# Infini-attention with a 2-D Fourier filter: stacks by 16-partition transfers, maxima eleven heads ahead, an output projection of 14 products

## The chip, the cores and the metric

The kernel runs on one core of one Trainium2 chip. The metric is the device time of one execution in microseconds, the median of the runs. A core has TensorE (PE for its products, PEld for its weight loads), VectorE (DVE), ScalarE (ACT), GpSimd (POOL) and SyncE (SP, which issues most transfers), and 16 DMA engines that carry the transfers of all issue queues.

## The reference

Two independent computations, whose results stand side by side in the output. `A` is an attention with a compressive memory, `B` filters in the frequency domain.

```python
# A: B=1, S=2048, D=576, H=32 heads of Dh=18, N=4 segments of L=512
q,k,v = heads(x@wq), heads(x@wk), heads(x@wv)
phi = lambda t: where(t > 0, t + 1, exp(t))
M, z = 0, 0
for s in range(N):
    p     = softmax(qs @ ks.T * Dh**-0.5 + mask)       # causal inside a segment
    a_dot = p @ vs
    a_mem = (phi(qs) @ M) / (phi(qs) @ z + 1e-6)
    o     = g * a_mem + (1 - g) * a_dot                # g = sigmoid(beta), one per head
    M    += phi(ks).T @ vs;   z += sum(phi(ks))
y_a = concat_heads(o) @ wo
# B: x is 2048 x 576
y_b = irfft2(rfft2(x) * (w_r + 1j*w_i))
```

## The kernel before

**Precision.** Products that need float32 are made of several passes: each operand is split into a high part with a short mantissa and the rest, a low part, and high x high, high x low and low x high are added up. The scores are made in one bfloat16 product of 108 rows: q and k are each split into three bfloat16 parts, and a *stack* holds six blocks of 18 rows (one block for each pair of parts), for eight heads and the 512 columns of a segment. Rows 108 and 109 of the query stack hold the row's maximum in two parts; rows of -1 in the key stack take it off inside the product, so that the exponential needs no subtraction.

**Stages.** The program runs the forward transform of `B`, then the projections of `A` beside the filter's pointwise part, then the inverse transform beside the first part of the attention (`prologue`), and then the attention. `projections` runs, for each of four segments, nine units of `qk_unit` (128 columns of q or k each, 1152 in all; the fifth unit, `mt==4`, is half q and half k) and four of `v_unit`. A `qk_unit` writes its three bfloat16 parts to DRAM (`qkD`), phi(q) to DRAM (`pqD`), and phi(k), transposed, to the tile `pk`.

**The attention's loop.** `attention` runs 133 steps, one head a step; four heads are a group (`k`, with head `hh` in it), eight a stack (`n`), and there are 16 stacks. Step `t` holds

- `s1(t+10)`: the scores of the head ten further on, four products and a reduction to each row's maximum on VectorE. The part on the diagonal is masked on TensorE by adding a triangle (L646, reduced by a plain reduction L647) for two of the four row blocks, and by a fused mask-and-maximum on VectorE (L641) for the other two.
- `mpath(k+2)`: for a group of four heads, the maxima are split on GpSimd (L662, L663), transposed on TensorE (L666), copied (L669) and sent into rows 108 and 109 of the query stack (L672), by a transfer from ScalarE's queue two steps later. It begins in the group's second head (`hh==1`) and goes on in its fourth (`hh==3`).
- `s2(t)`: the transposed scores with the maximum taken off, the exponential on ScalarE, and GpSimd's selection of the causal part once per group (L696).
- `pv`: the products P x V of the group before, in two of four steps, and `u_dmas`, which write the sums to DRAM.
- a share of the background list `bg`: loading and splitting `wo` (`late_setup`), and for each finished segment `mixed` (the memory part `mem1`, and `combine`, which scales, adds and splits into the high part `oh` and the low part `ol`), `den` (the denominators of the next segment), and `oproj`, the output projection.

**Order.** The order on every engine's queue is that in which the Python generators emit instructions; a wait on a queue holds up everything behind it. SyncE's queue gets up to two stack, value or sum transfers a step from the lists `q` and `qu`. `stack_dmas(n, qk)` is the list of the six transfers of a stack, 18 rows each (L621). When stack `n` begins, the transfers of the query stack `n+2`, of the key stack `n+3` and of the values are appended. There are three query and four key buffers, so a query buffer comes free when the last head of stack `n-1` is through `s2`. Requests made with `later(d, ...)` go out `d` steps later.

**The output projection.** The 576 rows of `o` lie in five tiles: four of 126 rows (seven heads) and one of 72 (four heads). `oproj` makes, for each of four row blocks and two halves, 15 products (three pairs of parts by five tiles), for the first three segments. The fourth segment's projection is `last_proj`, in an order of its own.

Of the kernel before, what the change touches and what calls it, by code (L numbers as in the profile page):

```python
# [340 lines left out]
BF=mybir.dt.bfloat16  # L341
H=32; DH=18; SC=float(DH)**-0.5
# [15 lines left out]
def host_wo(w):  # L358
    o=np.zeros((126,5,D),np.float32)
    o[:,:4]=w[:504].reshape(4,126,D).transpose(1,0,2)  # L360
    o[:72,4]=w[504:]
    return o
# [21 lines left out]
class ATT:  # L384
    def __init__(s,nc,tc,io,cp,dp):
# [6 lines left out]
        s.qkD=[d(f"qkD{i}",[1152,3,512],BF) for i in range(4)]  # L392
        s.pqD=[None]+[d(f"pqD{i}",[576,512],F32) for i in range(1,4)]
# [67 lines left out]
    def qk_unit(s,g,mt,tp,pp):  # L461
# [18 lines left out]
        if qr>r0: nc.sync.dma_start(s.pqD[g][128*mt:128*mt+qr],e[:qr])  # L480
# [5 lines left out]
        nc.sync.dma_start(s.qkD[g][128*mt:128*mt+128],sp3)  # L486
# [3 lines left out]
        n=r1-k0; c0=128*mt+k0-576  # L490
# [4 lines left out]
        nc.scalar.copy(s.pk[:,:,c0:c0+n],pt[:,:,:n])  # L495
# [99 lines left out]
    def late_setup(s,cp):  # L595
# [3 lines left out]
        s.woh=cp.tile([126,5,576],F32R,name="woh",bufs=1); s.wol=cp.tile([126,5,576],F32R,name="wol",bufs=1)  # L599
        for t in range(6):  # L600
            if t>1: yield
            if t<5:
                x=cp.tile([128,576],F32,name="ob")[:126]; q.append(x)
                nc.sync.dma_start(x,io["wo"][:,576*t:576*t+576])
            for _ in range(2): yield
            if t>0:
                x=q.pop(0)
                nc.scalar.copy(s.woh[:,t-1],x)
                nc.gpsimd.tensor_tensor(s.wol[:,t-1],x,s.woh[:,t-1].bitcast(F32),op=OP.subtract)
        yield  # L610
        yield from s.gates()
    def stack_dmas(s,n,qk):

        nc=s.nc; g,G=divmod(n,4)
        L=[]
        T,base,order=((s.Qs[n%3],0,(0,0,0,1,1,2)),(s.Ks[n%4],576,(0,1,2,0,1,0)))[qk]
        for pc,o in enumerate(order):
            a=s.qkD[g][base+8*G*18:base+8*G*18+18,o]
            ap=bass.AP(tensor=a.tensor,offset=a.offset,ap=[[1536,18],[1536*18,8],[1,512]])
            def go(T=T,pc=pc,ap=ap):  # L620
                nc.sync.dma_start(T[18*pc:18*pc+18],ap)  # L621
                if pc==5: s.loaded.add((n,qk))
            L.append(go)
        return L
# [5 lines left out]
    def s1(s,t):  # L630
# [163 lines left out]
    def mixed(s,g):  # L794
# [3 lines left out]
        for i in range(5+d):  # L798
            next(c,None); yield
            if i>=d:  # L800
                for _ in s.mem1(g,i-d): yield
# [4 lines left out]
    def combine(s,g):  # L806
# [14 lines left out]
        for t in range(7+late):  # L821
# [13 lines left out]
            if late and t>2: low(t-3)  # L835
# [288 lines left out]
```

## Time and profile before

| | us |
|---|---|
| median of three runs (726.09, 726.72, 837.55) | 726.72 |
| the profiled execution | 718.92 |
| its span, first to last instruction | 717.2 |

The granted clock of TensorE over the span is 0.997. The busiest groups of VectorE in the attention, in busy time and mean duration: the fused mask-and-maximum L641, 256 times, 141.4 us and 552 ns; the plain reduction L647, 128 times, 87.7 us and 686 ns. Of the output projection, TensorE's three groups on L849 have 120 products each. The stack transfers are 192 with 144.0 KB each.

How to read the page: "busy" is the union of an engine's instructions; matmuls are pipelined, so their mean duration is longer than the distance between two of them. A wait names the engine that was idle, the line it waited at, and what ended the wait. The chain is followed back from the last instruction through whatever released each step.

### The profile page before, as it was taken

How to read it: one execution, taken by the hardware profiler on the slowest of the kernel's cores; microseconds unless marked ns; L12 is line 12 of the kernel's file. 1: busy time of each engine (PE TensorE's matmuls, PEld its weight loads, DVE VectorE, ACT ScalarE, POOL GpSimd, SP SyncE). 2: the span in 40 equal slices, each digit the busy share in tenths (PEclk: the TensorE clock that was granted, in tenths of full speed). 3: DMA queues.
4: the chain of work that ended last, by engine and by line, in shares of the span. 5: the costliest groups of instructions: out<-in, count | busy, mean ns of one | idle time of the engine just before them, and what ended most of it. 6: DMA issues, size and time to landing. Idle time of an engine off the chain costs nothing. (4 is left out here: it accounts for less than half of the span.)

```text
span 717.2 us, 14460 instructions
## 1 busy us (share of the span) xinstructions
PE 684.1 (95%) x5007; PEld 505.7 (71%) x5007; DVE 552.3 (77%) x1270; ACT 450.1 (63%) x985; POOL 211.1 (29%) x403
## 2 busy tenths in 40 slices
PE   4999999999999999999999899899999999999997
PEld 4988869879779879999854444444466445664497
DVE  5999979899699789788588787878466876568633
ACT  3665796585586575444487677767466776567521
POOL 5432000100200111665154333435123662235300
PEclk9999999999999999999999999999999999999999
DMA  8995435645363568899547665776446775441152
GB/s 305 293 280 164 148 118 185 192 169 182 110 220 147 178 198 281 208 231 228 165 111 174 171 172 136 185 173 170 114 126 158 195 169 126 126 137 42 28 153 83
DMA packets 83304, 121.02 MB, mean 169 GB/s; under 512 B 11472, under 2 KB 50750, under 8 KB 83096
## 3 DMA queue, kind: packets, MB, share of 16 engines
q1 hardware_dynamic: 76580, 104.11, 50.3%
q0 software_dynamic: 5632, 15.76, 8.0%
q8 instruction: 39, 0.64, 0.4%
q10 hardware_dynamic: 1020, 0.25, 0.2%
q14 instruction: 33, 0.27, 0.1%
HBM read 81.78 MB, written 38.24 MB: 167 GB/s over the span
## 5 line engine op out<-in xcount | busy, mean ns | idle before, releaser
L641 DVE CUSTOM_DVE_ANT_0 junk<-s,x 128x512 bf16<-128x512 f32 (+1 forms) x256 | 141.4, 552 | 67.2 <-PE s L637 62.0
L696 POOL TENSOR_SCALAR_AFFINE_SELECT P<-P 128x512 f32<-128x512 f32 (+2 forms) x132 | 78.8, 623 | 67.3 <-ACT P L683 51.8
L647 DVE TENSOR_REDUCE mx<-s 128x4 f32<-128x512 f32 x128 | 87.7, 686 | 2.9 <-PE s L646 0.7
L683 ACT ACTIVATE P<-s 128x512 f32<-128x512 f32 x128 | 76.4, 597 | 16.5 <-PE s L682 5.4
L711 PE MATMUL pv<-P,vs 128*32 128x512 f32 (+3 forms) x1024 | 82.8, 441 | 0.0
L692 ACT ACTIVATE P<-s 128x256 f32<-128x256 f32 x128 | 49.4, 386 | 49.7 <-PE s L691 49.6
L688 ACT ACTIVATE P<-s 128x512 f32<-128x512 f32 x128 | 76.1, 594 | 2.0 <-PE s L687 1.8
L637 PE MATMUL s<-Ks,Qs 108*128 108x384 bf16 (+3 forms) x256 | 69.1, 301 | 1.2 <-DVE mx L647 0.9
L711 PEld LDWEIGHTS pv<-P,vs 128*32 128x32 f32 x1024 | 27.2, 109 | 45.3 <-issue 42.5
L459 PE MATMUL pj<-x,wqkh 128*128 128x512 f32 x162 | 56.5, 409 | 0.0
L205 DVE TENSOR_TENSOR Z<-t,t 128x290 f32<-128x290 f32 (+1 forms) x96 | 48.4, 554 | 0.1
L637 PEld LDWEIGHTS <-Qs 108*128 108x128 bf16 x320 | 31.5, 98 | 22.6 <-issue 11.3
L506 POOL MEMSET vt<- 128x32 f32 x16 | 2.4, 166 | 149.1 <-PE pm L516 127.7
L205 DVE TENSOR_TENSOR t<-Z 128x580 f32<-128x580 f32 x64 | 46.0, 755 | 0.0
L142 PE MATMUL f<-ftab,eh 128*128 128x290 f32 (+1 forms) x160 | 32.5, 322 | 12.1 <-DMA ftab<-ftab 9.5
L646 PE MATMUL s<-tri,idb 128*128 128x128 bf16 x256 | 43.2, 220 | 0.0
L295 PE MATMUL i<-civ,Y 128*128 128x256 f32 (+1 forms) x288 | 39.0, 288 | 0.2 <-POOL Y L280 0.2
L295 PEld LDWEIGHTS i<-civ,Y 128*128 128x128 f32 (+1 forms) x288 | 36.4, 181 | 1.0 <-POOL Y L280 0.4
L306 PE MATMUL i<-itab,T 128*128 128x290 f32 (+1 forms) x224 | 36.3, 305 | 0.1
L637 PE MATMUL s<-Ks,x 108*128 108x384 bf16 (+3 forms) x128 | 35.3, 306 | 1.1 <-DVE mx L647 0.6
L142 PEld LDWEIGHTS f<-ftab,eh 128*128 128x128 f32 (+1 forms) x160 | 26.2, 207 | 14.1 <-issue 8.5
L459 PE MATMUL pj<-x,wqkl 128*128 128x512 f32 x90 | 35.5, 395 | 0.0
(203 smaller groups left out, 1820.8 us busy)
## 6 DMA issues: line engine op xcount, KB each, us to landing
qkD<-sp SPq DMA_DIRECT2D x36, 384.0 KB
Ks<-qkD SPq DMA_DIRECT2D x72, 144.0 KB
x<-qkD SPq DMA_DIRECT2D x60, 144.0 KB
Qs<-qkD SPq DMA_DIRECT2D x60, 144.0 KB
xin<-xb SPq DMA_DIRECT2D x16, 384.0 KB
cfw<-cfw POOLq DMA_DIRECT2D x16, 384.0 KB, 4.4
civ<-civ POOLq DMA_DIRECT2D x16, 384.0 KB, 7.6
vs<-vD SPq DMA_DIRECT2D x16, 330.0 KB
```

What stands on the lines that cost most here:

```text
L142: nc.tensor.matmul(p[:,r,:FP],x,t,start=n==0,stop=n==6)
L205: v.tensor_tensor(o,a,b,op=op)
L295: nc.tensor.matmul(p[:m,k],Y[i][:,q,c*128:c*128+m],cc[:,hl,o:o+256],start=n==0,stop=n==5)
L459: s.nc.tensor.matmul(out,a,b,start=i==0,stop=i==len(L)-1)
L637: nc.tensor.matmul(out,Q[:108,h,128*i:128*i+128],K[:108,h,:128*(i+1)],start=True,stop=True)
L641: nc.vector.tensor_tensor_reduce(out=junk[:,:w],in0=src,in1=s.mask[:,512-w:],scale=1.0,scalar=-3.0e38, op0=OP.add,op1=OP.max,accum_out=s.m ...
L647: nc.vector.tensor_reduce(out=s.mx[k][:,hh],in_=pa.rearrange("p (b c) -> p b c",c=128),axis=mybir.AxisListType.X,op=OP.max)
L683: nc.scalar.activation(P[0][:,hh],p0,AF.Exp,scale=SC)
L688: nc.scalar.activation(P[1][:,hh],p1,AF.Exp,scale=SC)
L692: nc.scalar.activation(P[2][:,hh],p2,AF.Exp,scale=SC)
L696: nc.gpsimd.affine_select(out=x[:,r],in_=x[:,r],pattern=[[0,r.stop-r.start],[1,128]],compare_op=OP.is_ge,fill=0.0,base=0,channel_multiplie ...
L711: nc.tensor.matmul(s.pvt[32*hh:32*hh+32,128*j:],vt[:,j,19*h:19*h+32],mv[0][:,hh,mv[1]],start=j==0,stop=j>1,skip_group_check=True)
```

## The change

*Layout.* The columns of `wq` and `wk` are permuted on the host, so that a unit of 128 columns holds dimensions 0 to 15 of eight heads (dimension by dimension), and the unit `mt==4` holds dimensions 16 and 17 of all heads, of q and of k. A stack then has six blocks of 16 rows, which come from `qkD`, and twelve rows of the last two dimensions, which unit `mt==4` writes ready in order to a new DRAM tensor `reD` (six writes in place of one). The writes to `pqD` and the copies into `pk` undo the permutation by their access patterns.

*Order in the attention.* `s1` runs eleven heads ahead (the prologue eleven heads in place of ten), `mpath` begins in a group's first head and goes on in its second, and four heads (11 to 14) take the triangle and the plain reduction for all row blocks. The loads `ux` of the reciprocal's lane are asked for before its own loads, the tiles of `combine` and `mem1` are taken in the order 4, 0, 1, 2, 3, and four steps of `oproj` come ahead of `den`.

*Projection.* For the first three segments the tile of 72 rows is filled up: rows 72 to 127 of its high part and rows 72 to 87 of its low part get the low part by small copies between tiles, with matching rows of `wo`, so that its three products become two.

```diff
+ORD=(4,0,1,2,3)
 # qk_unit
-        nc.sync.dma_start(s.qkD[g][128*mt:128*mt+128],sp3)
+        if mt!=4: nc.sync.dma_start(s.qkD[g][128*mt:128*mt+128],sp3)
+        else:
+            for r,i,c,n in ((0,0,1,3),(0,1,1,2),(0,2,1,1),(64,0,3,3),(64,0,2,2),(64,0,1,1)):
+                m={3:0,2:3,1:5}[n]; a=s.reD[g][r*12//64+2*m]
+                x=sp3[r:r+64,i:i+c] if c==n else sp3[r:r+64,i:i+1].to_broadcast([64,n,512])
+                nc.sync.dma_start(bass.AP(tensor=a.tensor,offset=a.offset,ap=[[512,64],[64*512,n],[1,512]]),x)
...
-        nc.scalar.copy(s.pk[:,:,c0:c0+n],pt[:,:,:n])
+        pk=s.pk.rearrange("p a (h d) -> p a d h",d=18)
+        if mt==4: nc.scalar.copy(pk[:,:,16:],pt[:,:,:n].rearrange("p a (d h) -> p a d h",d=2))
+        else: nc.scalar.copy(pk[:,:,:16,8*mt-40:8*mt-32],pt.rearrange("p a (d h) -> p a d h",h=8))
 # stack_dmas
-            a=s.qkD[g][base+8*G*18:base+8*G*18+18,o]
-            ap=bass.AP(tensor=a.tensor,offset=a.offset,ap=[[1536,18],[1536*18,8],[1,512]])
-            def go(T=T,pc=pc,ap=ap):
-                nc.sync.dma_start(T[18*pc:18*pc+18],ap)
-                if pc==5: s.loaded.add((n,qk))
-            L.append(go)
+            a=s.qkD[g][base+128*G,o]
+            ap=bass.AP(tensor=a.tensor,offset=a.offset,ap=[[1536*8,16],[1536,8],[1,512]])
+            L.append(lambda pc=pc,ap=ap: nc.sync.dma_start(T[16*pc:16*pc+16],ap))
+        def go():
+            nc.sync.dma_start(T[96:108],s.reD[g][12*qk:12*qk+12,8*G:8*G+8])
+            s.loaded.add((n,qk))
+        L.append(go)
 # s1, red
+            if 11<=t<15:
+                nc.tensor.matmul(src[:,w-128:w],s.idb,s.tri,start=False,stop=True,skip_group_check=True)
+                nc.vector.tensor_reduce(out=s.mg[k][:,hh,i:i+1],in_=src,axis=mybir.AxisListType.X,op=OP.max)
+                return
 # combine, low
-            eng().tensor_tensor(s.ol[u][:r],s.am[u][:r],s.oh[u][:r].bitcast(F32),op=OP.subtract)
+            A,B=s.oh[u],s.ol[u]
+            l=B if u<4 else tp.tile([128,512],F32R,name="ol4",bufs=1)
+            eng().tensor_tensor(l[:r],s.am[u][:r],A[:r].bitcast(F32),op=OP.subtract)
+            if u==4:
+                s.later(1,lambda: nc.sync.dma_start(B[:72].bitcast(F32),A[:72].bitcast(F32)))
+                s.later(2,lambda: (nc.sync.dma_start(A[72:128].bitcast(F32),l[:56].bitcast(F32)),nc.sync.dma_start(B[72:88].bitcast(F32),l[56:72].bitcast(F32))))
 # oproj
-                L=[(a,b,t) for a,b in ((oh,s.woh),(oh,s.wol),(ol,s.woh)) for t in range(5)]
+                L=[(a,b,t,126) for a,b in ((oh,s.woh),(oh,s.wol),(ol,s.woh)) for t in range(4)]+[(oh,s.woh,4,128),(ol,s.wol,4,88)]
 # prologue
-        for t in range(10):
+        for t in range(11):
             for _ in s.s1(t):
-                for _ in range(1+(i%24==0)):
+                for _ in range(1+(i%5==0)):
 # attention
                     for i in range(8):
+                        if 2<i<6: s.ux_load(g-1,ORD[i-3])
                         next(r); yield
-                    for u in range(3): s.ux_load(g-1,u)
                     yield from r
                     bg.append(s.mixed(g))
-                    if g<3: bg.append(s.den(g+1,lane))
-                    bg.append(s.oproj(g-1))
+                    o=s.oproj(g-1)
+                    if g<3: bg.append(itertools.islice(o,4)); bg.append(s.den(g+1,lane))
+                    bg.append(o)
...
-            a=s.s1(t+10) if t+10<128 else iter(())
+            a=s.s1(t+11) if t+11<128 else iter(())
...
-            if hh==3 and m is not None: steps(m,1)
+            if hh==1 and m is not None: steps(m,1)
             steps(b,1)
-            if hh==3 and m is not None: steps(m,1)
-            if hh==1 and k+2<32: m=s.mpath(k+2); next(m)
+            if hh==1 and m is not None: steps(m,1)
+            if hh==0 and k+2<32: m=s.mpath(k+2); next(m)
```

The rest of the diff is the host's permutation and layout of the weights, one more row block of `wo` loaded in `late_setup`, tiles of 128 rows in place of 126, and the order 4, 0, 1, 2, 3 where tiles are loaded.

More of the change, by code (lines that the diff above doesn't have):

```diff
@@ L392, in __init__ @@
         s.qkD=[d(f"qkD{i}",[1152,3,512],BF) for i in range(4)]
+        s.reD=[d(f"reD{i}",[24,32,512],BF) for i in range(4)]
         s.pqD=[None]+[d(f"pqD{i}",[576,512],F32) for i in range(1,4)]
@@ L598, in late_setup @@
         s.sel=cp.tile([96,5,126],BF,name="sel",bufs=1); nc.gpsimd.dma_start(s.sel,io["sel"].rearrange("p (t m) -> p t m",t=5))
[L599 to L603, printed above, removed]
-                nc.sync.dma_start(x,io["wo"][:,576*t:576*t+576])
[L605 to L609, printed above, removed]
+        s.woh=cp.tile([128,5,576],F32R,name="woh",bufs=1); s.wol=cp.tile([128,5,576],F32R,name="wol",bufs=1)
+        for t in (0,1,2,3,5,4,6):
+            if t: yield
+            if t<6:
+                x=cp.tile([128,576],F32,name="ob"); q.append((t,x))
+                nc.sync.dma_start(x,io["wo"][:,576*t:576*t+576])
+            yield
+            if t!=5: yield
+            if len(q)>(t<6):
+                u,x=q.pop(0)
+                if u==5: nc.scalar.copy(s.wol[64:96,4],x[64:96]); continue
+                r=128 if u<4 else 72
+                nc.scalar.copy(s.woh[:,u],x)
+                nc.gpsimd.tensor_tensor(s.wol[:r,u],x[:r],s.woh[:r,u].bitcast(F32),op=OP.subtract)
         yield
```

52 lines of the change are left out of this document (29 added, 23 removed).

## The prediction

> **What bounds the kernel now.** I read the page first, then the busy time by stage, then the waits of TensorE in the attention, then the chain and the DMA rows of one stage, and last single rows for prices.
>
> ```profile
> span 717.2 us, 14460 instructions
> PE 684.1 (95%) x5007; PEld 505.7 (71%) x5007; DVE 552.3 (77%) x1270; ACT 450.1 (63%) x985; POOL 211.1 (29%) x403
> ```
>
> TensorE is busy 95% of the span, so time goes only where it does less work or waits less. The stages, with PE, PEld, DVE, ACT and POOL busy, clock, DMA share and GB/s:
>
> ```profile
> 80.00:280.00 200.00, 198.01 (x1128) 167.87 (x1127) 174.03 (x327) 137.52 (x272) 14.27 (x62) 1.00 0.55 181
> 280.00:345.00 65.00, 64.77 (x517) 61.48 (x516) 53.04 (x125) 30.74 (x75) 36.49 (x54) 1.00 0.84 213
> 345.00:677.00 332.00, 317.96 (x2663) 178.26 (x2662) 241.61 (x691) 226.69 (x544) 127.94 (x233) 0.99 0.55 142
> 372.00:410.00 38.00, 34.64 (x318) 17.43 (x316) 30.19 (x95) 28.25 (x69) 16.42 (x29) 1.00 0.70 171
> 410.00:440.00 30.00, 29.95 (x277) 14.82 (x268) 24.17 (x76) 23.01 (x56) 10.04 (x22) 1.00 0.56 151
> 440.00:512.00 72.00, 66.10 (x541) 32.11 (x539) 55.31 (x160) 50.70 (x121) 28.71 (x55) 0.98 0.69 170
> 677.00:717.00 40.00, 35.47 (x261) 33.44 (x261) 14.62 (x23) 8.75 (x21) 2.92 (x6) 0.99 0.34 109
> ```
>
> Projections (80 to 280) and inverse transform (280 to 345) leave TensorE idle for 2.0 and 0.2 us. The attention (345 to 677) leaves it idle 332.0 - 318.0 = 14.0 us, of which 3.4 lie in 372:410 and 5.9 in 440:512. These two are also the stages with a DMA share near 0.7, and 440:512 has the one clock below 1. What ends TensorE's waits in the attention (total, times, longest):
>
> ```profile
> PE s L682 <- DMA Qs<-mts: 3.2, 3, 1.4
> PE s L637 <- DVE mx L647: 1.5, 4, 0.6
> PE pd L765 <- DMA pq<-pqD: 1.4, 1, 1.4
> PE pb L826 <- DMA rr<-rrD: 1.2, 1, 1.2
> PE s L637 <- DMA Qs<-qkD: 0.4, 1, 0.4
> PE s L682 <- DMA x<-mts: 0.2, 1, 0.2
> ```
>
> Five of the six are transfers: 3.2 + 1.4 + 1.2 + 0.4 + 0.2 = 6.4 us. The chain of waits shows how long they take (start, duration):
>
> ```profile
> 372.67 7.55 DMA Qs<-mts
> 387.69 5.19 DMA pq<-pqD
> 392.89 8.27 DMA Qs<-qkD
> 401.24 5.59 DMA x<-mts
> 408.17 0.06 PE s L646
> ```
>
> The maxima (mts, 32 x 128 bfloat16, 8 KB) take 7.55 us, as long as a stack transfer, so they stand in a queue. The DMA rows of 410:440, where almost only stacks are loaded, show which queue (first line: busy share in 40 slices; then packets, MB and share; then issues):
>
> ```profile
> DMA  6667666666666656986566666566642002252255
> q1 hardware_dynamic: 4584, 4.43, 54.5%
> Ks<-qkD SPq DMA_DIRECT2D x12, 144.0 KB
> SPq L621 <- DMA Ks<-qkD: 12.3, 14, 1.6
> ```
>
> The last line is a wait of SP's issue queue in 345 to 700: stack issues (L621) wait for earlier stack transfers, so transfers are always pending, yet the 16 engines are pinned near 0.6. Eighteen rows divide evenly over nine engines with two rows each; 9/16 is 0.56, near the measured 54.5% and the flat run of sixes. I read it as nine full engines and seven idle ones. [...]
>
> **The change part by part.** *Stacks.* Six transfers of 18 rows become six of 16 (one row per engine) and one of 12. By rows, an engine among the nine did 6 x 2 = 12 rows per stack and now does at most 7: 7/12 of the load. The queueing part of 5 to 8 us should shrink alike, to 3 to 5 us. That bears on all DMA-ended waits.
>
> *Maxima two heads earlier.* The transpose and its store move from the fourth head of a group to the second, and the request from the second to the first, possible because the scores run one head further ahead. A pair of heads takes as long as from one P x V block (L711) to the next. Rows of this stretch (start, duration), and GpSimd groups (total, mean ns):
>
> ```profile
> 410.83 0.16 DVE L659 TENSOR_REDUCE mg<-mx 128x4 f32<-128x12 f32 x1
> 411.47 0.22 POOL L663 TENSOR_TENSOR mh<-mg,mh 128x16 bf16<-128x16 f32 x1
> 412.88 1.28 PE L711 MATMUL pv<-P,vs 128*32 128x384 f32 x16
> 416.72 0.08 DVE L641 DVE_READ_ACCUMULATOR2_ANT mg<- 128x1 f32 x1
> 416.92 0.64 PE L711 MATMUL pv<-P,vs 128*32 128x512 f32 x4
> ```
>
> ```profile
> L819 POOL TENSOR_TENSOR ol<-am,oh 126x512 fp32r<-126x512 f32 (+1 forms) x10 | 12.7, 1270 | 16.4 <-ACT oh L816 15.4 <-PE pn L784 1.0
> L832 POOL TENSOR_TENSOR am<-ux,am 126x512 f32<-126x512 f32 (+1 forms) x8 | 10.1, 1273 | 4.5 <-DVE ux L831 3.3 <-PE s L682 1.2
> ```
>
> 416.92 - 412.88 = 4.04 us, so the maxima get 4 us more, three times the longest wait for them (1.4). The 3.4 us for mts go. The waits for pq and rr go too: four steps of the output projection now stand between the last pq load and its use, and the ux loads no longer stand in the queue ahead of rr. I take all 6.4 us. What is late next is VectorE: its waits already stand in the list (1.5 us), and I give back 1.0 (bounds: 0; all 6.4).
>
> The price of the earlier transpose: TensorE takes instructions in order, and matmuls of the next head's scores and exponentials queue behind it. The last maximum of the group is now that of the first head of four, out of VectorE at 416.72 in the rows above; from the reduction L659 to the end of L663 is 411.69 - 410.83 = 0.86 us, giving 417.6. The transpose follows the P x V block that starts at 416.92 and takes 1.28 us: 418.2, a margin of 0.6. Where one of GpSimd's 1.27 us operations (L819, L832, second fence) lies in between, it is late by some 0.7. Of these 18 a quarter falls in that step: 4.5 x 0.7 = 3.2 at most; I take 1.5 (bounds 0 and 3.2).
>
> *Clock.* 440:512 ran at 0.98, costing 72 x 0.02 = 1.4 us. It is the stage with the pq wait of 1.4 us, the longest; I let it go with the wait (bounds 0 and -1.4). [...]
>
> *Products.* 3 segments x 8 tiles lose one product of 15:
>
> ```profile
> 683.70 0.83 PE L849 MATMUL po<-wol,oh 126*128 126x288 f32 x5
> 684.37 0.83 PE L849 MATMUL po<-woh,ol 126*128 126x288 f32 x5
> ```
>
> Five products start every 0.67 us, 0.134 each; 24 x 0.134 = 3.2 us. Sixteen lie in the full stages 512:560 and 600:650 and count whole, 2.1. Eight lie after 677, where the last segment's tiles wait for loads anyway (TensorE 35.5 of 40); I take 0.5 of their 1.1. So -2.6 (bounds -2.1, -3.2). The nine small copies that fill rows 72 to 127 are asked for when tile 4 is combined, which now comes first, some ten steps (20 us) ahead of its products; they cost nothing while those steps cover them.
>
> *First four heads.* Before the first P x V block VectorE sets the pace, and TensorE waits for it (L637 on L647, above):
>
> ```profile
> 356.18 0.69 DVE L647 TENSOR_REDUCE mx<-s 128x4 f32<-128x512 f32 x1
> 357.39 0.08 DVE L641 DVE_READ_ACCUMULATOR2_ANT mg<- 128x1 f32 x1
> 357.62 0.42 DVE L641 CUSTOM_DVE_ANT_0 junk<-s,x 128x256 bf16<-128x256 f32 x1
> 357.97 0.69 DVE L647 TENSOR_REDUCE mx<-s 128x4 f32<-128x512 f32 x1
> ```
>
> A head takes 1.79 us, of which 0.23 pass between the accumulator read and the next operation. A plain reduction has no such read: 4 x 0.23 = -0.9 (bound 0). The eight mask products added (0.06 each by the L646 piece of the chain, 0.5) fall in TensorE's waits.
>
> *One head moved* from the attention into the inverse transform: TensorE is full in both, so 0 (bounds: one step, 2.0, either way).
>
> *Projections.* Twenty more SP issues and a permuted copy on ScalarE:
>
> ```profile
> L621 SPq DMA_DIRECT2D Ks<-qkD x72: 265/273/468, 301.5 to 607.9; - x72
> L495 ACT COPY pk<-ptr x15: 357/588/622, 100.5 to 225.5; 128x512 f32<-128x512 f32 x12, 128x256 f32<-128x256 f32 x3
> ```
>
> Twenty issues at 0.27 us are 5.4 us of SP in 200; behind them queue the tables and inputs, loaded ahead. The copies write single words 72 bytes apart, which no row shows; if each took twice its 588 ns, ScalarE had 15 x 0.59 = 8.8 us more on 137.5 of 200. TensorE at 99% covers both. Uncovered it were +8.8; I take 0.
>
> **Sum.** -6.4 + 1.0 + 1.5 - 1.4 - 2.6 - 0.9 = -8.8 us. The profiled execution took 718.92 us (717.2 and 1.7 around it), so 710.1; the median of the runs is 726.72, 1.1% higher for no cause in the rows, and the same difference gives 717.9.
>
> **Rivals.** *A, the forecast*, 713 to 722: chance 0.61. *B, VectorE takes the place of the transfers.* Waits vanish into its own; only the products count, 726.7 - 2.6 = 724. For it: VectorE is at 55.3 of 72 in 440:512, and a head took it 1.79 of 2.02 us. Against: 410:440 ran with no transfer wait and no idle TensorE. 0.15. *C, all idle time goes*: -14.0 - 3.2 - 1.4 = -18.6, 708. For it: VectorE, too, has operands sooner. Against: a third of the listed waits is not for transfers. 0.14. *D, slower: query stacks come late.* The slot of a query stack comes free when its eighth head is done; then five steps (10.1 us) pass until its first scores instead of six, and seven transfers must be issued, not six. If 16 rows land no sooner than 18, that is one step and one issue interval (about 1 us) less: 3.1 us per stack, 13 stacks, +40, so 758. It is slower than before beyond 8.8/13 = 0.7 us per stack, and by 2% beyond 1.8. For it: the wait on Qs<-qkD exists already, with 8.27 us in the chain. Against: the 54.5%. [...] 0.08. *E*, the ScalarE copies uncovered, 727: 0.02.
>
> **Numbers.** 2%, about what a measurement here tells from no change, is 14.5 us: faster below 712.2, slower above 741.3. Only C is faster by that, 0.14; only D slower, 0.08; 0.78 within. The range 708 to 728 holds A, B, E and half of C: 0.85.
>
> **What would show it.** Right: TensorE's waits on Qs<-mts, pq and rr gone; DMA share in the attention unlike 0.56 and spread over time; stack transfers landing in 3 to 5 us in the chain; L849's successor with 336 products; idle time in the attention near 9 us (14.0 - 6.4 + 1.0 + 1.5 - 0.9). Wrong: TensorE waiting on Qs<-qkD once per stack (D), on GpSimd at the transpose once per group, on VectorE where transfers were (B), or idle in the projections (E).

## The result, and the profile after

The changed kernel takes 732.03 us (median; 730.67 to 736.75), the kernel before on the same chip 726.33 (one of its six runs took 837.55). All ratios of this document are formed over undisturbed runs alone, so that of the change, 1.0134 with a 95% interval of 1.0087 to 1.0182, isn't the quotient of these medians. It is slower, by less than 2% but clear of the noise, and outside the range given. In the experiments that follow the kernel before took 719.6 to 722.4 us (medians), so each is told by its ratio to the kernel before in the same series, with the interval.

The page of the profiled execution after, and the time by stage (columns as in the prediction's table). The two profiled executions lie 13 us apart, a little more than the ratio says:

```profile
span 730.2 us, 14514 instructions
PE 685.9 (94%) x4991; PEld 502.8 (69%) x4991; DVE 552.9 (76%) x1262; ACT 457.5 (63%) x986; POOL 209.8 (29%) x403
```

```profile
80.00:280.00 200.00, 196.64 (x1117) 166.33 (x1116) 171.84 (x322) 142.35 (x269) 14.14 (x60) 1.00 0.62 186
280.00:345.00 65.00, 63.21 (x505) 59.83 (x504) 54.85 (x125) 30.79 (x76) 35.08 (x54) 1.00 1.08 211
372.00:410.00 38.00, 29.88 (x256) 14.52 (x255) 25.14 (x80) 24.74 (x60) 16.66 (x28) 0.92 0.81 160
410.00:440.00 30.00, 28.74 (x253) 14.29 (x255) 22.77 (x70) 20.91 (x51) 8.46 (x18) 0.92 0.75 140
440.00:512.00 72.00, 65.31 (x535) 31.67 (x528) 53.32 (x158) 48.97 (x117) 27.14 (x52) 0.95 0.80 156
512.00:560.00 48.00, 48.00 (x407) 30.47 (x405) 30.97 (x90) 31.41 (x76) 13.80 (x28) 1.00 0.73 153
```

Two things stand out. The stretch 372 to 512 has become the worst: TensorE's clock is 0.92 to 0.95 there, and 410:440, which had no idle TensorE before, has some. And in the four stages shown from 280 to 512 the DMA share has risen while the GB/s have fallen (410:440: 0.56 and 151 before, 0.75 and 140 now). The transfers keep the engines busy longer for fewer bytes.

Where the time is lost shows in the times at which the same instruction runs in both traces (us from the start of each span, read from the instruction records):

```
event                                        before   after   later by
last product of the projections              282.04  283.25     1.2
last product of the inverse transform        355.35  358.77     3.4
first product of s2 of head 16               388.09  392.13     4.0
                      of head 24             406.96  418.07    11.1
                      of head 40             440.51  452.48    12.0
                      of head 56             477.32  495.04    17.7
                      of head 120            659.04  672.78    13.7
first product of the last projection         696.13  708.72    12.6
end                                          717.23  730.15    12.9
```

There are three main losses: 3.4 us up to the end of the inverse transform, 7.1 between heads 16 and 24, and 5.7 between heads 40 and 56. TensorE's waits in the attention after (total, times, longest; Qs and Ks are the buffers of the query and key stacks, x the tile that holds the first of each and the mask, mts the maxima):

```profile
PE s L702 <- ACT P L703: 6.6, 7, 4.8
PE s L653 <- DMA ux<-uD: 3.8, 1, 3.8
PE mt L686 <- POOL mh L683: 2.6, 5, 0.8
PE s L653 <- DVE mg L679: 2.0, 1, 2.0
PE s L653 <- DMA uD<-U: 1.4, 1, 1.4
PE s L653 <- DMA Qs<-qkD: 1.3, 1, 1.3
```

The waits on mts, pq and rr are gone. In their place stand single waits of 4.8, 3.8 and 2.0 us. A wait for several things carries the name of one of them, so the transfers themselves have to be looked up. The stack around the wait of 3.8 us, which ended at 465.5 (asked, landed, from the DMA records):

```
Qs<-qkD  454.81 456.04 456.62 457.26 457.91 458.55   landed 459.00 460.27 461.26 462.20 463.28 464.20
Qs<-reD  459.22                                      landed 465.19
```

It is the query stack: its seventh transfer lands at 465.19. The wait of 2.0 us ends at 485.21, and the last part of the next query stack landed at 485.02. At the wait of 4.8 us, which ended at 406.4, a query stack is late as well (last part asked 400.37, landed 408.35), but ScalarE's own queue stands still until 405 (a row of ScalarE's waits in 372 to 410, and a piece of its timeline):

```profile
ACT P L703 <- DMA pq<-pqD: 6.4, 1, 6.4
```

```profile
405.06 0.62 ACTq L692 DMA_DIRECT2D x<-mts  x1
```

ScalarE issues the request for the maxima at 405.06, 0.1 us after a pq load landed (404.98); the exponentials behind it in its queue wait, and TensorE waits for them. Why it stands there is in the instruction records. The program marks the landing of SyncE's and ScalarE's transfers in eight semaphores (counters that an engine can wait for), in turn: the 638 requests of the two queues use each of them 79 or 80 times, and none goes out before the transfer that had its semaphore before has landed. The request for the maxima has the semaphore of the pq load asked for at 396.05, the one that landed at 404.98. So these two queues together have at most eight transfers under way (eight is the highest count in this trace and in that of the kernel before), and slow landings hold back the requests behind them: SyncE's next two stack requests, at 460.29 and 461.27, went out as the parts in the list above landed, at 460.27 and 461.26.

Each of the three stalls comes with a clock at half of full speed, 10.2 us from 404.3 and 3.4 us each from 465.7 and 486.2 (ten microseconds a row):

```profile
400.00:410.00 10.00, 4.77 (x34) 2.15 (x27) 3.87 (x12) 3.27 (x9) 2.82 (x6) 0.71 0.88 162
410.00:420.00 10.00, 10.00 (x75) 4.78 (x74) 6.27 (x19) 6.14 (x16) 2.40 (x4) 0.77 0.52 134
460.00:470.00 10.00, 6.11 (x41) 2.62 (x40) 5.31 (x16) 4.66 (x13) 3.95 (x11) 0.83 1.05 157
480.00:490.00 10.00, 8.02 (x64) 3.62 (x64) 6.36 (x18) 5.05 (x12) 4.08 (x7) 0.83 0.98 171
```

Over 372 to 512 the clock costs 38 x 0.08 + 30 x 0.08 + 72 x 0.05 = 9.0 us, against 1.4 before.

### The profile page after: what moved, and what is told of

Read it like the earlier page. It is cut to its first block, busy times and chain, and to the rows that moved or that the text cites. A ratio compares the mean times of both kernels' runs of the same rounds, so it can differ in the third digit from the quotient of the medians.

```text
span 730.2 us, 14514 instructions
## 1 busy us (share of the span) xinstructions
PE 685.9 (94%) x4991; PEld 502.8 (69%) x4991; DVE 552.9 (76%) x1262; ACT 457.5 (63%) x986; POOL 209.8 (29%) x403
## 4 chain that ended last, share of the span: by engine, by line
PE 51%; DMA 7%; ACT 2%; SPq 2%; issue 2%; POOL 2%; DVE 2%; ACTq 0%; POOLq 0%; DVEq 0%
PE s L653 8%; PE pv L731 8%; PE i L295 5%; PE po L874 5%; PE i L306 4%; PE pj L461 4%; PE s L702 3%; PE pjv L461 3%; PE s L706 2%; PE po L903 2%; DMA ux<-uD 2%; PE pn L804 2%; PE s L666 2%; SPq L635 2%; PE s L711 1%
## 5 line engine op out<-in xcount | busy, mean ns | idle before, releaser
L661 DVE CUSTOM_DVE_ANT_0 junk<-s,x 128x512 bf16<-128x512 f32 x248 | 136.9, 552 | 68.5 <-PE s L653 63.6
L703 ACT ACTIVATE P<-s 128x512 f32<-128x512 f32 x128 | 77.5, 605 | 26.2 <-PE s L702 12.7
L731 PE MATMUL pv<-P,vs 128*32 128x512 f32 (+3 forms) x1024 | 85.5, 452 | 0.1
L708 ACT ACTIVATE P<-s 128x512 f32<-128x512 f32 x128 | 77.2, 603 | 2.9 <-PE s L707 2.7
L205 DVE TENSOR_TENSOR Z<-t,t 128x290 f32<-128x290 f32 (+1 forms) x96 | 49.7, 567 | 0.1
L205 DVE TENSOR_TENSOR t<-Z 128x580 f32<-128x580 f32 x64 | 46.0, 755 | 0.0
```

The lines of the kernel that those rows point to most:

```text
L205: v.tensor_tensor(o,a,b,op=op)
L661: nc.vector.tensor_tensor_reduce(out=junk[:,:w],in0=src,in1=s.mask[:,512-w:],scale=1.0,scalar=-3.0e38, op0=OP.add,op1=OP.max,accum_out=s.m ...
L703: nc.scalar.activation(P[0][:,hh],p0,AF.Exp,scale=SC)
L708: nc.scalar.activation(P[1][:,hh],p1,AF.Exp,scale=SC)
L731: nc.tensor.matmul(s.pvt[32*hh:32*hh+32,128*j:],vt[:,j,19*h:19*h+32],mv[0][:,hh,mv[1]],start=j==0,stop=j>1,skip_group_check=True)
```

## The experiments

The first four expectations name four theories of the late query stacks: P, the place (16 neighbouring partitions are filled slowly); H, the row pitch in DRAM; Q, the budget (eleven heads ahead leave a stack one step less, rival D of the prediction); S, ScalarE's request that stands behind a pq load.

**1. Rows of a transfer spread over 96 partitions**

```diff
-nc.sync.dma_start(T[16*pc:16*pc+16],ap)
+nc.sync.dma_start(T[pc:96:6],ap)
```

> The changed kernel, with the sixteen rows of a stack transfer written to every sixth partition (0, 6, 12, ... of the first 96) in place of sixteen neighbours; queries and keys alike, so the product is the same. [...] Theory H (pitch): the sixteen source rows lie 24 KB apart in DRAM and collide there; nothing changes, 728 to 735. Theory Q (budget): the transfers' pace is not the matter, only that a query stack has one step less and one transfer more; nothing changes, 728 to 735.

**2. Another pitch in DRAM**: rows of 1,600 elements instead of 1,536.

```diff
-s.qkD=[d(f"qkD{i}",[1152,3,512],BF) for i in range(4)]
+s.qkD=[d(f"qkD{i}",[1152,1600],BF) for i in range(4)]
```

> The changed kernel, with the rows of the DRAM tensor of the three parts padded from 3072 to 3200 bytes, so that the sixteen source rows of a transfer lie 25.6 KB apart in place of 24.6. Theory H (pitch): stack transfers land in about 3.5 us and the time falls to 708 to 718. Theories P (place) and Q (budget): no change, 728 to 735.

**3. The maxima requested from GpSimd's queue**

```diff
-s.later(2,lambda: nc.scalar.dma_start(out,mt))
+s.later(2,lambda: nc.gpsimd.dma_start(out,mt))
```

> The changed kernel, with the maxima's transfer asked for on GpSimd's queue in place of ScalarE's. Theory S (semaphore): ScalarE's request stood 6.4 us behind a transfer of another tensor, which held up the exponentials, TensorE (4.8 us) and then the clock (10.2 us at half); with the request elsewhere this stall goes with its clock drop, and the time falls by 6 to 10 us, to 722 to 726. Theory P (place) alone: the same transfers are late, TensorE waits at that place for the query stack instead, and the time falls by 0 to 4 us. GpSimd pays about 0.65 us for each of 30 requests, off the path.

**4. The kernel before with its 18 rows spread**

```diff
-nc.sync.dma_start(T[18*pc:18*pc+18],ap)
+nc.sync.dma_start(T[pc:108:6],ap)
```

> The kernel before, with the eighteen rows of a stack transfer written to every sixth partition of 108. [...] The prediction's theory (nine engines are full): nine engines carry the same rows, no change, within 2 us of 726.

Measured: spread 1.1019 (1.0942 to 1.1097); pitch 1.0119 (1.0048 to 1.0189); maxima from GpSimd 1.0200 (1.0138 to 1.0261); before spread 1.1247 (1.1188 to 1.1306). H falls: nothing changed. S falls as the cause of the loss: with GpSimd asking, ScalarE no longer stands still for a transfer, but TensorE then waits for the stack itself, and longer (its waits in 372 to 520):

```profile
PE s L653 <- DMA Ks<-qkD: 7.9, 1, 7.9
PE s L653 <- DMA x<-qkD: 4.2, 1, 4.2
PE s L653 <- DMA Qs<-reD: 2.7, 1, 2.7
```

The two spread kernels are slower than with neighbouring rows, which seems to refute P, but their pages hold a wait that has nothing to do with the speed of a transfer (the group of the mask-and-maximum in the spread kernel, with its idle time and what ended it):

```profile
L661 DVE CUSTOM_DVE_ANT_0 junk<-s,x 128x512 bf16<-128x512 f32 x248 | 137.3, 554 | 133.9 <-DMA x<-qkD 71.1
```

VectorE waits 71 us for stack transfers that this instruction doesn't read. It reads the mask, and the mask lies in one tile (x0) with the first query and the first key stack. With every sixth partition written, readers of the tile's other parts wait as well. So these two runs say nothing on P, and the next ones give the mask a tile of its own.

**5 and 6. Spread rows with tiles of their own, and the control**

```diff
-t=pool.tile([128,9,512],F32,name="x0",tag="x0",bufs=1)
+t=[pool.tile([128,4 if i<2 else 1,512],F32,name=f"x{i}",tag=f"x{i}",bufs=1) for i in range(3)]
...
-nc.sync.dma_start(T[16*pc:16*pc+16],ap)
+nc.sync.dma_start(T[pc:96:6],ap)
```

> The changed kernel with two edits: the 16 rows of a stack transfer go to every sixth of 96 partitions, and the mask and the first query and key stacks get tiles of their own (in the first spread kernel VectorE's mask reads waited 71 us for stack writes to the tile that they share). P (place: 16 neighbouring partitions take rows slowly, 1.0 to 1.2 us per transfer however many engines write; spread ones take them faster): key stacks land in about 3 us in the attention instead of 4.1, query stacks in 3 to 4 instead of 5.5; the three stalls of TensorE on late query stacks (about 12 us) and the slow clock behind them (about 7 us) go; 712 to 720 us. Q (budget: query stacks are late because the scores run eleven heads ahead and so leave one step less, whatever the landing): the stalls shrink by at most the landing gain, 2 us each; 724 to 730. F (the strided destination itself costs, apart from the shared tile): over 760.

The control has the first half of this edit alone.

> The changed kernel with tiles of their own for the mask and the first two stacks, and nothing else: the control for the spread kernels. If the gain of those is in the place of the rows: as the changed kernel, 1.010 to 1.018 of the kernel before. If it is in the tiles: 1.002 to 1.006, as the spread kernel.

**7. The same in the kernel before** (18 rows to `T[pc:108:6]`, tiles of their own)

> The kernel before with the same two edits: its 18 rows go to every sixth of 108 partitions. P: it lands sooner here too although the number of engines stays at nine; the waits for mts, pq, rr and Qs<-qkD (6.4 us) shrink by half or more; 716 to 722 us. If only the number of engines counted, landing and time stay as in the kernel before, 726. F (a strided destination costs): over 760.

Measured: spread 1.0042 (0.9990 to 1.0094), control 1.0162 (1.0110 to 1.0215), kernel before spread 0.9875 (0.9792 to 0.9959). The control stands where the changed kernel stands, so the gain of run 5 is in the place of the rows. Its time, 724.4 us, is nevertheless the one that Q expected, not P's 712 to 720, while the landings further down are as P expected; run 7 is where P expected it. The rows of SP's transfer queue on the pages (packets, MB, share of 16 engines' span) of the kernel before, the changed kernel, and the two with spread rows (5, then 7):

```profile
q1 hardware_dynamic: 76580, 104.11, 50.3%
```

```profile
q1 hardware_dynamic: 79270, 106.89, 59.2%
```

```profile
q1 hardware_dynamic: 79270, 106.89, 50.6%
```

```profile
q1 hardware_dynamic: 76580, 104.11, 46.2%
```

Share x 16 engines x span / MB is the engine time that a megabyte takes: 0.503 x 16 x 717.2 / 104.11 = 55.4 us before; 64.7 after (span 730.2); 54.5 for run 5 (719.1); 50.3 for run 7 (708.6). The change made a megabyte dearer by 17%. These rows cover all that SP asks for, of which the stacks are about a quarter (28 of 104 MB). The stacks' own packets, 1 KB each, can be told in the DMA records: from 365 to 515 one takes 66 ns in the mean before, 90 in the changed kernel, 59 in run 5 and 53 in run 7. The medians from request to landing (transfers into Ks and Qs):

```
us, requests at             key stacks           query stacks
                         280-365  365-515      280-365  365-515
kernel before              9.99     6.10         8.79     6.38
changed kernel             8.48     4.07         8.31     5.53
changed, spread (5)        4.92     3.06         4.34     3.96
before, spread (7)         6.52     4.39         5.06     4.64
```

From one landing of a stack transfer to the next, 1.13 us pass in the kernel before and 1.00 in the changed kernel (medians, requests from 365 to 515); P had named 1.0 to 1.2 for neighbouring rows.

SP's own time for a stack request isn't what makes the kernel slower: a key stack's takes 0.27 us before and 0.55 in the changed kernel, but 0.76 in run 7, which is the faster one.

By what the place of the rows acts, the runs don't show, only that it counts; and sixteen spread rows are only a little cheaper than eighteen neighbours (54.5 us a megabyte against 55.4, 59 ns a packet against 66).

In the kernel with 18 spread rows the chain through the attention holds no transfer of a stack or of maxima any more (of transfers, rrD and rr are left, 5.2 and 4.2 us), and the waits on mts and pq are gone with nothing but place and tiles changed; the longest wait on a transfer that is left:

```profile
PE pb L826 <- DMA rr<-rrD: 0.9, 1, 0.9
```

**8 and 9. Ten heads ahead again, alone and with the spread rows**

```diff
-if 11<=t<15:
+if 10<=t<14:
...
-a=s.s1(t+11) if t+11<128 else iter(())
+a=s.s1(t+10) if t+10<128 else iter(())
...
-if hh==1 and m is not None: steps(m,1)
+if hh==3 and m is not None: steps(m,1)
...
-if hh==0 and k+2<32: m=s.mpath(k+2); next(m)
+if hh==1 and k+2<32: m=s.mpath(k+2); next(m)
```

> The changed kernel with the scores ten heads ahead again and the maxima's transpose and store at their old places; stacks, output projection and order of loads as changed. Q (budget): each query stack has its sixth step back, 2.0 us; the stalls on query stacks fall from about 12 us to under 3 and the slow clock with them; 718 to 724 us. P (place): the transfers are as slow as before the edit, and the stall at 400 us, 4.8 and 2 us late, stays in part; 724 to 729. If neither, 732 as the changed kernel.

> Both: ten heads ahead, and the spread stacks with tiles of their own. If place and budget both count, this is the fastest: no wait for a stack is left, 710 to 716 us. If place alone counts, as the spread kernel with eleven heads, within 2 us. If budget alone counts, as the kernel with ten heads, within 2 us.

Measured: ten heads 1.0064 (1.0023 to 1.0106), both 0.9955 (0.9918 to 0.9992). Place and budget both count and add up: 0.9 to 1.2% for the place (run 5 against the changed kernel and against the control, run 9 against run 8), 0.7 to 0.9% for the budget. With both, 717.9 us, the time isn't as low as expected (710 to 716). In run 8 one stall stays, as P said, 5.6 us that end at 410.2; the seventh part of the query stack, asked for at 403.15, landed at 409.83. The late stacks at 465 and 485 are gone. At 465.8 a wait of 1.8 us is left, for ScalarE, which again stood before a request for the maxima until a transfer with the same semaphore had landed.

**16 and 17. Eleven heads in a kernel with six fast transfers.** The budget alone is best seen where nothing else is late. The base is run 13 below (the kernel before, spread, with the output projection's part; 0.9814). Run 16 adds the eleven heads with the earlier maxima and the four heads with the plain reduction, run 17 the eleven heads with the maxima at their old steps.

> The kernel before with spread stacks of 18 rows, the output projection's part, and now also the scores eleven heads ahead with the maxima's transpose and store earlier. The same kernel ten heads ahead stood at 0.9814. Q (one step less for a query stack costs whatever the kind of transfer): TensorE waits on query stacks again, 0.985 to 0.992. P (with transfers that land in 4.6 us the budget of five steps is enough): 0.978 to 0.982, with the waits on maxima gone and GpSimd's transposes 2 to 3 us instead.

> The kernel with spread stacks of 18 rows and the output projection's part, scores eleven heads ahead (0.9971 with the earlier transposes, 0.9814 ten heads ahead), with the maxima's transpose and store left at their old steps. Q (the one step that query and key stacks lose is the price): TensorE still waits some 7 us for stacks; only the 2.7 us of waits on GpSimd at the transposes go; 0.990 to 0.995. M (the earlier transposes are the price, in waits and in what they push back): 0.980 to 0.984.

Measured: 0.9971 (0.9945 to 0.9996) and 0.9961 (0.9929 to 0.9993), 1.6% and 1.5% above the base. TensorE's waits in the attention of the base, of run 16 and of run 17:

```profile
PE s L686 <- ACT P L687: 2.7, 4, 1.9
PE s L641 <- DVE mx L651: 1.5, 4, 0.6
```

```profile
PE s L641 <- DMA Ks<-qkD: 3.6, 2, 2.6
PE mt L674 <- POOL mh L671: 3.0, 6, 0.8
PE s L641 <- DMA Qs<-qkD: 2.3, 1, 2.3
PE s L641 <- DMA x<-qkD: 1.4, 1, 1.4
```

```profile
PE s L641 <- DMA Qs<-qkD: 4.2, 1, 4.2
PE s L641 <- DMA x<-qkD: 2.4, 1, 2.4
```

No wait on a stack with ten heads, 7.3 us in run 16, 6.6 in run 17: Q is right, with a price above the one expected, and M falls. The transposes cost 3.0 us, and leaving them at the old step brings nothing, since the stacks are late either way. SP's side of it is the time that stack requests wait for the slot to be read to the end (base, then run 16):

```profile
SPq L625 <- PE s L641: 16.3, 7, 3.5
```

```profile
SPq L625 <- PE s L641: 22.7, 10, 4.2
```

**10 and 11. The copies on ScalarE**

```diff
-pk=s.pk.rearrange("p a (h d) -> p a d h",d=18)
+pk=s.pk.rearrange("p a (h d) -> p a h d",d=18)
...
-else: nc.scalar.copy(pk[:,:,:16,8*mt-40:8*mt-32],pt.rearrange("p a (d h) -> p a d h",h=8))
+else: nc.scalar.copy(pk[:,:,8*mt-40:8*mt-32,:16],pt.rearrange("p a (d h) -> p a h d",h=8))
```

> The changed kernel with one edit: the pk copies on ScalarE run through the elements in the order in which they are written (16 words in a row, then the next head), and read the transpose's bank with a stride instead; same data, same places. C (the copies are the cause of the 3.4 us by which the inverse transform ends later): the copies fall from 1096 ns to under 800, the projections end 1 us sooner, VectorE's last butterflies no longer lie under GpSimd's subtraction at 286 us, TensorE's wait of 1.8 us there goes; inverse ends at 355.5 to 356.5 instead of 358.8; 727 to 730 us. R (the stores and issues added to SP, or something else, set the projections back): the copies get shorter, projections and inverse end as before the edit, 732. T (the slow part is reading with a stride, or the number of short runs, not the place of the written words): copies stay near 1100.

> Ten heads ahead, spread stacks with tiles of their own, and the copies in the order of the written words. C: 3 to 5 us under the kernel without the last of these (717.86): 712 to 715. R and T: within 1 us of it.

Measured: 1.0189 (1.0115 to 1.0262) and 0.9937 (0.9907 to 0.9966). The copies by themselves (min/median/max ns; the changed kernel, then run 10):

```profile
L507 ACT COPY pk<-ptr x12: 1021/1096/1128, 103.7 to 226.3; 128x512 f32<-128x512 f32 x12
```

```profile
L507 ACT COPY pk<-ptr x12: 573/597/633, 104.1 to 225.6; 128x512 f32<-128x512 f32 x12
```

Writing single words 72 bytes apart took 1.84 times as long; with 16 words in a row the price is gone although the reads now have a stride. T falls. The projections end at 282.2 again, as C said, but the time doesn't fall as C expected: the inverse now ends at 361.1, not at 355.5. A wait at its start has grown by 1.8 us, and the clock stands at half for 3.4 us behind it, which costs another 1.7 (TensorE's waits, the changed kernel and run 10):

```profile
PE i L295 <- ACT T L332: 1.8, 1, 1.8
```

```profile
PE i L295 <- issue: 3.6, 1, 3.6
```

**14 and 15. The stores of the two remaining dimensions issued by GpSimd** (run 11 and run 10 with this edit)

```diff
-nc.sync.dma_start(bass.AP(tensor=a.tensor,offset=a.offset,ap=[[512,64],[64*512,n],[1,512]]),x)
+nc.gpsimd.dma_start(bass.AP(tensor=a.tensor,offset=a.offset,ap=[[512,64],[64*512,n],[1,512]]),x)
```

> Ten heads ahead, spread stacks with own tiles, copies in the order of the written words, and the 24 stores of the two remaining dimensions (reD) issued by GpSimd instead of SP. S (SP's queue: six reD stores of 0.6 to 0.7 us stand ahead of the store of a projected tile, the tile's buffer comes free late, ScalarE waits 0.99 us for it, VectorE's last butterflies slip under GpSimd's subtraction and are stretched from 0.45 to 1.4 us and more, TensorE waits 3.6 to 3.9 us): ScalarE's wait and TensorE's wait of 3.9 at 287 us go; the inverse ends at 355 to 356 instead of 361.2; 5 us under the kernel without this edit (0.9937 of the kernel before): 0.985 to 0.988. N (the stretch of the butterflies has another cause, such as the stack loads in the projections): inverse ends at 360 and more, 0.992 to 0.995.

> The changed kernel with the copies in the order of the written words and the reD stores on GpSimd's queue; stacks, heads ahead and projection as changed. S: projections and inverse end as in the kernel before (282 and 355 to 356), the attention with its late query stacks as in the changed kernel; 3 to 4 us under it: 1.007 to 1.010 of the kernel before. N: as the kernel with the copies alone, 1.014 to 1.019.

Measured: 0.9899 (0.9867 to 0.9932) and 1.0211 (1.0164 to 1.0257). The first lies between what S and N expected, with an interval that overlaps run 11's; the second is above both. The inverse ends at 360.1 and 363.1, the projections at 283.7 and 283.1, later than in runs 11 and 10 (281.7 and 282.2), and the wait at the start of the inverse is still there (1.9 and 3.9 us, where runs 11 and 10 have 3.9 and 3.6). SP's queue as the cause isn't borne out.

**18. The subtraction beside VectorE's last butterflies.** In run 11, at the start of the inverse, GpSimd subtracts (L280) while VectorE does its last butterflies (L205). Here VectorE does the first of those subtractions itself, behind its butterflies.

```diff
-if u+2<16: s.ysplit(u+2)
+if u+2<16: s.ysplit(u+2,v if u==0 else None)
```

> Ten heads ahead, spread stacks with own tiles, copies in the order of the written words (0.9937), and the first subtraction of the inverse transform that GpSimd did (L280 at 286 us) done by VectorE after its last butterflies. G (VectorE's last butterflies are stretched, 0.45 to 1.4 and 1.8 us, because GpSimd's subtraction runs beside them): they take 0.45 each again, VectorE pays 1.1 us for the subtraction, TensorE's wait of 3.9 us at 287 falls under 2; 0.988 to 0.991. L (the stretch has nothing to do with GpSimd): the butterflies stay at 1.4 us, the wait at 3.9 or 5; 0.993 to 0.996.

Measured: 0.9900 (0.9857 to 0.9942), as G expected, though the interval overlaps run 11's. VectorE's last five butterflies (min/median/max ns, first and last start) in the kernel before, in run 11 and in run 18:

```profile
L205 DVE TENSOR_TENSOR Z<-t,t x5: 452/455/756, 282.9 to 285.0; 128x290 f32<-128x290 f32 x3, 128x580 f32<-128x580 f32 x2
```

```profile
L205 DVE TENSOR_TENSOR Z<-t,t x5: 755/826/1819, 283.8 to 287.3; 128x290 f32<-128x290 f32 x3, 128x580 f32<-128x580 f32 x2
```

```profile
L205 DVE TENSOR_TENSOR Z<-t,t x5: 451/453/755, 284.1 to 286.2; 128x290 f32<-128x290 f32 x3, 128x580 f32<-128x580 f32 x2
```

G is right by these rows. Three butterflies of 0.45 us took 1.45, 0.83 and 1.82 us in run 11 beside GpSimd's subtraction, and 0.45 each without it; TensorE's wait fell from 3.9 to 1.4 us, and the half clock behind it went. From the last product of the projections to the last of the inverse it is 73.3 us before, 75.5 in the changed kernel, 79.5 in run 11 and 74.4 in run 18. In the kernel before, the butterflies start a microsecond earlier, and the last has just begun when GpSimd starts its subtraction (285.0 and 285.08).

**12 and 13. The output projection's part alone**: in the kernel before, and in the spread kernel before (run 7).

```diff
-L=[(a,b,t) for a,b in ((oh,s.woh),(oh,s.wol),(ol,s.woh)) for t in range(5)]
+L=[(a,b,t,126) for a,b in ((oh,s.woh),(oh,s.wol),(ol,s.woh)) for t in range(4)]+[(oh,s.woh,4,128),(ol,s.wol,4,88)]
...
-if 16<=t<21: s.pq_load(1,t-16)
+if 16<=t<21: s.pq_load(1,ORD[t-16])
```

> The kernel before with the output projection's part of the change alone: 14 products for three segments, their order of loads, the small copies that fill rows 72 to 127; stacks, heads ahead and projections as before. By the forecast's term: 2.6 us less for 24 products and some 2 us less of waits on pq and rr, so 3 to 5 us under the kernel before. Rival: the added copies and the other order cost as much as the products give: within 1 us of the kernel before. If this part is the loss, slower by 3 us and more.

> The kernel before with spread stacks (18 rows to every sixth of 108 partitions, tiles of their own) and the output projection's part of the change. The spread kernel before stood at 0.9875 of the kernel before. If the products add to it: 2.5 us less, 0.984; the waits on rr and pq are gone there already. If the projection's part costs: 0.99 and more.

Measured: 1.0031 (0.9992 to 1.0069) and 0.9814 (0.9757 to 0.9871). With slow transfers the products bring nothing: in run 12 TensorE waits 8.1 us on ScalarE and 5.8 us on mts and query stacks in the attention, and ScalarE itself stands five times before a request for the maxima, 1.4 to 3.6 us each. With spread transfers the part takes the kernel from 0.9875 to 0.9814, with intervals that overlap. Run 13 is the fastest of all, 706.95 us where the kernel before took 719.63; its stages:

```profile
372.00:410.00 38.00, 38.00 (x352) 19.19 (x351) 32.65 (x103) 31.24 (x76) 18.69 (x35) 1.00 0.67 203
410.00:440.00 30.00, 29.94 (x270) 14.92 (x268) 24.17 (x74) 22.77 (x56) 9.79 (x20) 1.00 0.49 148
440.00:512.00 72.00, 68.20 (x576) 36.01 (x575) 56.11 (x165) 51.64 (x125) 28.68 (x54) 1.00 0.58 172
```

The clock is full in all three, and 372:410 has no idle TensorE.

## Why the prediction was wrong

- **Stacks: the step that failed.** "7/12 of the load" counted engines and took the rows' speed as fixed. No run shows the 7/12, nor how many engines carry a transfer: nine and seven idle ones were the author's reading of the 54.5%. The records mark the landing of 16 rows sixteen times where 18 rows had ten marks, which fits more engines, and a key stack's part did land in 4.1 us instead of 6.1. But a stack's packet of 1 KB took 90 ns instead of 66, a query stack's part landed in 5.5 us instead of 6.4, and there are seven parts. The flat 0.56 of DMA share was read as nine engines at their limit; run 7, with the same 18 rows spread, has 0.47 in the same stage, so part of it was where the rows went.
- **Rival D, given 0.08, is what happened**, with its price mis-sized. Its condition (16 rows land no sooner than 18) was put as all or nothing; the lost step costs even where a query stack's parts land in 4.1 to 4.4 us (medians of runs 17 and 16, 365 to 515; 1.5 and 1.6%), and 0.7 to 0.9% in the changed kernel (run 8 against it, run 9 against run 5). It doesn't cost 3.1 us on each of 13 stacks: three stalls of 2 to 5 us, and then the clock. D didn't foresee that ScalarE would stand in the longest of them. The share of 54.5%, held against it, doesn't say how fast rows are taken.
- **Waits that end with a transfer, -6.4:** the listed ones went, as said. What is late next was sought in VectorE (+1.0); it was the stacks.
- **Transposes, +1.5:** the mechanism was right, the size 2.6 us in five waits, inside the bounds. The wait on VectorE's L679 (2.0 us) is a late stack by its landing.
- **Clock, -1.4:** wrong in sign, 7.6 us more in 372 to 512. In the kernel before the clock stood at half from 508.1 to 511.5, right behind the pq wait of 1.4 us that ended at 507.1, and that went as forecast; the three new stalls brought three others. The length of a wait alone doesn't settle whether the clock falls: waits of 1.4 us (440:512 before, at 0.98) and 2.0 us (480:490 after, at 0.83) were followed by a fall, one of 1.8 us at the start of the changed kernel's inverse transform brought none.
- **Products, -2.6:** about right. L849's successor has the 336 products that were announced. From head 56 to head 120 the changed kernel wins 4.0 us back, a stretch that holds the sixteen products of two segments (-2.1) and the kernel before's half clock (-1.7); run 13 against run 7 gives 0.6%, with intervals that overlap, so the size isn't shown better than that. Alone, beside slow transfers, they bring nothing (run 12).
- **First four heads, -0.9:** heads 0 to 8 take 15.1 us instead of 15.6. Right in sign and half the size, if the whole difference is this term's.
- **Projections, 0:** wrong by 3.4 us. "TensorE at 99% covers both" overlooked that no slack was left to cover with. The copies cost 1.1 us of projections (run 10). Of the inverse's 2.2 us, 0.4 are the products of the eleventh head (the moved head, put at 0) and 1.6 are the grown wait at its start. This wait fits VectorE's last butterflies, a microsecond late and then stretched beside GpSimd to 1.45 and 0.83 us, a term that the prediction didn't have; run 18 shows it on run 11, not on the changed kernel itself. The 24 requests for `reD` took 0.6 us each, not 0.27.
- **Readings.** "A third of the listed waits is not for transfers" (rival C) is 1.5 of 7.9 us, a fifth.

Three things stay open. What sets VectorE back by about a microsecond in the changed projections isn't settled: GpSimd's issuing of the extra stores moved the delay and didn't remove it. No run gives the maxima's request a semaphore of its own on ScalarE's queue, so what the shared one costs by itself isn't measured. And runs 11, 14 and 18 stand at 0.990 to 0.994 where run 13 stands at 0.9814. In the profiles of runs 18 and 13, 8.2 us apart at the last projection, 2.5 lie before the attention, and 5.4 fit one late key stack of run 18 (a wait of 3.7 us and 3.4 us at half clock); whether the seventh transfer of a stack makes it late, or the packets that stay dearer with spread rows too (59 ns against 53), wasn't separated.

## What to carry to other kernels

Before splitting a load over more DMA engines, ask where its rows land: rows on neighbouring partitions took longer here (90 and 66 ns for a packet of 1 KB, 59 and 53 with the rows spread), and spreading them gained 1.2% in the kernel before (interval 0.4 to 2.1%), with tiles of their own as the only other edit. Running a producer further ahead of its consumer takes the same step away from every buffer that is refilled behind it (1.6 and 1.5% in runs 16 and 17); look up who waits for the slot before moving it. And an engine that is a microsecond late at the border of two stages can meet another engine's work there that it used to miss (butterflies of 0.45 us took up to 1.82 in run 11), so check what runs beside the tail of each stage that is lengthened.

## What the runs showed of the hardware

- Engine time per megabyte on SP's queue, stacks and all else: 64.7 us with stack transfers to 16 neighbouring partitions, 55.4 to 18, 54.5 with 16 spread over 96, 50.3 with 18 spread over 108. A 1 KB packet of the stacks, from 365 to 515: 90, 66, 59 and 53 ns. The pitch of the DRAM rows (3,072 or 3,200 bytes) made no difference (1.0119 against 1.0134).
- A ScalarE copy of 128 x 512 float32 took 1096 ns when it wrote words 72 bytes apart and 597 ns when it wrote 16 words in a row.
- A VectorE subtraction or addition of 128 x 290 float32 took 0.45 us alone and up to 1.82 us beside a GpSimd subtraction.
- TensorE's granted clock fell to half with single waits of 2.0, 3.8 and 4.8 us (for 3.4, 3.4 and 10.2 us), in the kernel before behind one of 1.4 us (3.4 us). Behind one of 1.8 us in the changed kernel it didn't.
